# Attention and Fourier mixing on one core: the second batch's key maps, four places for the combinations of w_ch2, and a hold on the third batch's keys

## The chip, the cores and the metric

The kernel runs on one core of a Trainium2 chip. The metric is the device time of one launch in microseconds (us); smaller is better. All arithmetic is in f32.

## The reference, cut to what matters

There are 8 batches (B), 8 heads (H), 576 tokens (S) and a width of 512 (D, 64 per head).

```python
q_s = exp(q - max(q, -1)); q_s /= q_s.sum(-1) + 1e-9        # over the 64 columns of a head
k_s = exp(k - max(k, 2));  k_s /= k_s.sum(2) + 1e-9         # over the 576 tokens
kv  = einsum('bhsd,bhse->bhde', k_s, v)
x   = einsum('bhsd,bhde->bhse', q_s, kv)                    # then heads side by side: (B, S, 512)
u   = x + real(fft(fft(x, axis=1), axis=2))
un  = (u - mean(u)) / sqrt(var(u) + 1e-6)                   # over the 512 columns
out = u + relu(un @ w_ch1) @ w_ch2                          # w_ch1 512 x 2048, w_ch2 2048 x 512
```

`w_ch1` and `w_ch2` arrive as 64-bit floating-point numbers, two 32-bit words each, and the kernel itself turns them into f32. A block of 128 rows by 512 such numbers is called "a word block" below; there are 32 of them, 0 to 15 for `w_ch1` and 16 to 31 for `w_ch2`.

## The kernel before, in words

**One batch.** A batch has two halves. Its *front* is the attention and the Fourier mixing. Keys come in four items per batch (two heads each): `k_load` (L476), the maximum and exponential (`k_exp`, L501), five transposes on TensorE that ScalarE copies to `ks` (`k_turn`, L512), and ten matmul passes whose result goes, scaled, to `kvr` (`k_times_v`, L526). Queries come in four tiles of 128 tokens: exponentials in `q_exp` (L562), transposes in `q_turn` (L584), products with `kvr` in `q_times_kv` (L608), which leaves `x` (L615). The remaining tokens go through `t_turn`, `t_fold` and `t_times_kv`. `transform` (L639) folds the four `x` tiles by sums and differences (`tokens_folded`, `columns_folded`, `by_frequency`, `columns_again`, L648 to L674) and multiplies them by cosine and sine tables in five blocks (`block`, L684; ScalarE copies each result to `Z` and `ZT`, L707 to L712). `second` and `mix_own` (L718, L753) make the second transform and add it to `x`. `norm` (L764) takes the statistics, normalizes, transposes into `unT` and, from batch 1 on, adds the combinations that a Strassen product needs.

The *back* is the two products with `w_ch1` and `w_ch2`. For batch 0 they are plain (`plain`, L826): 16 steps `up(f)` of four matmuls, then 64 steps of `down`, of one matmul each, in the order of `DOWN` (L78). For the later groups they are Strassen products (`strassen`, L854, `up`, `down`), whose combined weights are streamed from DRAM (`w1s`, `w2s`) by `load` (L397). These combinations are made once, beside batch 0's `down`, by `combine` (L366): 8 for `w_ch1`, 8 for `w_ch2`. Each takes sums and differences of four quarters on GpSimd and VectorE, puts the four new quarters in a *place*, and stores them to DRAM by SyncE's DMA queue. For `w_ch2` there are two places in turn, both in `w1sb` (L376).

**Order of the work.** Each batch's front is run beside the back of the one before it. Batch 0's front has nothing to stand beside; neither have batch 1's keys, which are loaded early and handled by `second_keys` (L441), in four items: `maxima`, `exps`, then the pipelined pair `k_turn`, `k_times_v`. L1057 runs, in this order: batch 0's attention, batch 1's maxima and exponentials, batch 0's transform and mixing, batch 1's key products, batch 0's norm. Beside `up` run the conversions of the word blocks; beside the 64 `down` steps run the last conversions, the combinations, and a list `side` with batch 1's queries, transform, mixing and norm. The list `gaps` (L1083) says how many `down` steps lie between two entries of `side`:

```python
side = one + two + norm(1)
gaps = [6] + [4] * (len(one) - 1) + [3] * 5 + [1] * 4 + [2] * (len(two) - 9) + [1] * 7
```

Here `one` has 7 entries (the query pipeline of batch 1) and `two` has 12 (four folds, five blocks, three mixes).

The program is written in this order, but the builder may put an instruction ahead on its engine's queue where it takes it to be ready earlier. The code therefore holds some instructions back by hand: `gate(t, raw)` (L467) and `wait_for` (L257) are tiny VectorE operations that read `t` and rewrite a few elements of `raw` unchanged, so that whatever reads `raw` comes after `t`. `hold` (L264) takes work tiles at the start and frees them later by a tiny copy in `free(f)`; a DMA into such a tile can't be issued before. Batch 2's first key and value tiles are freed after `up(15)`.

**Where word blocks lie.** A fetched word block is raw until converted (`fetch`, `convert`, L313 to L348: two ScalarE operations, two on VectorE, a last one on GpSimd). `WORDS_AT` (L75) gives each one's place: 0 to 7 are pairs of rows of the `w2sb` array, 8 to 10 are tiles that later hold `x`, and 11 to 13 are parts of the tile of `unT`, free once `up` is over. A block whose place was used before is fetched when the former block is converted. The last three blocks (29, 30, 31) are fetched after `up`.

**Keeping TensorE clocked.** In batch 0's folds, `warm` (L201) runs two matmuls into an unused PSUM tile after each of the four `columns_folded` steps (L659); they read the folded tile.

Of the kernel before, what the change touches and what calls it, by code (L numbers as in the profile page):

```python
# [40 lines left out]
F32 = mybir.dt.float32  # L41
# [32 lines left out]

WORDS_AT = [*range(8), 8, 9, 10, *range(3, 8), 0, 1, 2, 8, 9, 10, 4, 5, 6, 7, 8, 9, 10, 11, 12, 13]  # L75
ORDER = (1, 6, 5, 7, 2, 4, 3)
# [20 lines left out]
def pipelined(items, stages):  # L97


    def step(t):  # L100
        for s in range(len(stages) - 1, -1, -1):
            if 0 <= t - s < len(items):
                stages[s](items[t - s])

    return [lambda t=t: step(t) for t in range(len(items) + len(stages) - 1)]
# [17 lines left out]
class _Block:  # L123
# [140 lines left out]
    def hold(self):  # L264


        held = {12: [("q", D, 3)] * 3, 15: [("k", S, 2)] * 2 + [("v", NC * P, 2)] * 2}
        for f, some in held.items():
            for i, (tag, n, bufs) in enumerate(some):
                t = self.work.tile([P, n], F32, tag=tag, name=tag, bufs=bufs)  # L270
                self.nc.gpsimd.memset(t[0:1, 0:1], 0.0)
                some[i] = t[0:1, 0:1]

        def free(f):
            copy = self.nc.vector.tensor_copy
            for t in held.get(f, ()):
                copy(t, self.h0[0:1, f, 0:1])
            if f == NF - 1:
                copy(self.w1sb[0:1, :, 0:1], self.w1sb[0:1, :, 0:1])
        return free  # L280
# [85 lines left out]
    def combine(self, layer, p):  # L366
# [6 lines left out]
        if layer == 0 and p < 2:  # L373
            t = [temp("s1"), temp("u2")] if p == 0 else [temp("u3"), temp("s1")]
        else:
            a = p // 2 * 2 - 2 + NP * (p % 2) if layer == 0 else NP + 2 * (p % 2)  # L376
            t = [pairs(self.w1sb[:, a + i, :]) for i in range(2)]
        quarter = lambda i: w[:, p + NP * (i // 2), (i % 2) * HD:(i % 2 + 1) * HD]
# [11 lines left out]
        nc.sync.dma_start(to[:, second], two)  # L390
        if layer or p > 1:
            nc.sync.dma_start(to[:, 3:], self.w1sb[:, a:a + 2, :].rearrange("p a (s n) -> p (a s) n", s=2))
            return
# [47 lines left out]
    def second_keys(self):  # L441


        nc, V = self.nc, self.nc.vector
        items = [("k", 1, r) for r in range(NR)]
        m, rec = (self.small.tile([P, NR], F32, tag=n, name=n, bufs=1) for n in ("km1", "krec1"))

        def maxima():
            self.gate(self.at_start[2][0][:, 1, :], self.second_at[0][0:1, ::S])
            for it in items:  # L450
                self.k_load(it)
                V.reduce_max(m[:, it[2]:it[2] + 1], self.live[it][0], axis=AX.X, negate=True)
            self.gate(self.xpart(0, 1, 1), m[0:1, :])

        def exps():
            for it in items:
                k, i = self.live[it][0], slice(it[2], it[2] + 1)
                nc.scalar.activation(k, k, ACT.Exp, bias=m[:, i], accum_out=rec[:, i])
                self.live[it].append(rec[:, i])

            t = self.small.tile([P, 1], F32, tag="root", name="root", bufs=1)
            nc.scalar.activation(t[:], rec[:, NR - 1:], ACT.Sqrt)
            V.tensor_scalar(out=rec[:], in0=rec[:], scalar1=ATT_EPS, scalar2=None, op0=ALU.add)
            V.reciprocal(rec[:], rec[:])
        return [maxima, exps], pipelined(items, [self.k_turn, self.k_times_v])

# [172 lines left out]
    def transform(self, b):  # L639
# [14 lines left out]
        def columns_folded(some=range(4)):  # L654
            for i in some:
                e, op = ((V if b == 0 else G), ALU.add) if i < 2 else (V, ALU.subtract)
                t = eo[i]
                e.tensor_tensor(out=t[:, 1:HD], in0=t[:, 1:HD], in1=t[:, D - 1:HD:-1], op=op)
                if b == 0:  # L659
                    self.warm(t[:, 0:HD], 2)  # L660
# [57 lines left out]
    def second(self, z, zr, add):  # L718
# [14 lines left out]
        if self.turns == 1:  # L733

            self.gate(sn[:], self.second_at[0][0:1, ::S])
        two = self.halves()
# [265 lines left out]
def kernel(ctx: ExitStack, tc: tile.TileContext, q, kT, v, w1, w2, ft,  # L1002
# [27 lines left out]
    def norm(g):  # L1030
        def make():
            nexts[g], steps = blk.norm(g)
            return steps
        return late(make, 7)
# [12 lines left out]
    def round_blocks(some):  # L1047
        for i in some:
            convert(i)
            if i in after:  # L1050
                fetch(after[i])
# [3 lines left out]
    one, two = front(0)  # L1055
    keys, products = blk.second_keys()
    for step in one + keys + two + products + norm(0):  # L1057
        step()

    groups = [*range(B - 1), B, B - 1]  # L1060
    for order, g in enumerate(groups):
        loads = [] if g == 0 else None
        one, two = front(order + 1, loads) if order + 1 < B else (blk.later, [])
        if g == 0:
            up, down = blk.plain(0, nexts.pop(0))

            round_blocks(range(4))
            n = 2 * NF - 14
# [8 lines left out]
            for step in loads:  # L1077
                step()
            for i in range(3):
                fetch(2 * NF - 3 + i)  # L1080

            side = one + two + norm(1)
            gaps = [6] + [4] * (len(one) - 1) + [3] * 5 + [1] * 4 + [2] * (len(two) - 9) + [1] * 7  # L1083
            at = 0
# [69 lines left out]
```

## Time and profile before

| what | value |
|---|---|
| median of 3 runs | 1137.43 us (1136.49 to 1137.56) |
| the profiled execution's own time | 1136.85 us |
| its span in the profile | 1135.1 us |
| TensorE (PE) busy | 1096.6 us, 97% |
| VectorE (DVE) / ScalarE (ACT) / GpSimd (POOL) busy | 533.4 / 404.6 / 332.2 us |
| first matmul of `up(0)` (L835) | starts at 65.56 us |
| first matmul of `down` (L844) | starts at 122.15 us |
| last `down` matmul of batch 0 ends | about 198.6 us |
| first matmul of the Strassen part (L905) | starts at 202.09 us |

Positions are microseconds from the start of the profile's span. Engines are PE, PEld (weight loads of TensorE), DVE, ACT, POOL and SP (SyncE, whose queue issues most DMAs; "SPq" is the issue). A row of the timeline reads: start, duration, engine, source line, operation, output<-input, count, and in brackets how long the engine had been idle just before and what released it. "x8" on a row of L835 or L844 are passes: each f32 matmul shows as two. The profiled execution's span leaves 1.75 us of its time outside.

### The profile page before, as it was taken

The numbers are of one execution on the slowest core, as the hardware profiler recorded it, in microseconds if no ns is written. First come the engines' busy times: TensorE is split into PE (matmuls) and PEld (weight loads), VectorE is DVE, ScalarE is ACT, GpSimd is POOL, SyncE is SP. The second block draws the span as 40 slices with busy tenths as digits, with TensorE's granted clock in tenths as the row PEclk, the third lists the DMA queues.
The fourth block names the chain that finished last, engine by engine and source line by source line (L and its number), as shares of the span: only waits on it lengthen the run. The fifth ranks groups of instructions, "written<-read, shape, count | busy, mean of one in ns | idle before, by whom it ended". The sixth has DMA issues, their size and how long they took to land.

```text
span 1135.1 us, 14578 instructions
## 1 busy us (share of the span) xinstructions
PE 1096.6 (97%) x5448; PEld 916.9 (81%) x5448; DVE 533.4 (47%) x1094; ACT 404.6 (36%) x975; POOL 332.2 (29%) x304
## 2 busy tenths in 40 slices
PE   5789999999999999999999999999999999999997
PEld 4644455888888988888889888888889888888886
DVE  6675756368434724384344733592434352203201
ACT  6595523355233513371325322451334152201200
POOL 2055462235003610334024402260034213402320
PEclk9899999999999999999999999999999999999999
DMA  9557675555346534544356425552453344444451
GB/s 312 166 190 227 244 272 161 169 208 167 113 156 215 182 140 144 194 158 177 122 178 220 149 103 183 190 198 107 144 191 150 113 154 160 175 150 151 156 185 55
DMA packets 92549, 193.79 MB, mean 171 GB/s; under 512 B 23088, under 2 KB 59696, under 8 KB 85312
## 3 DMA queue, kind: packets, MB, share of 16 engines
q1 hardware_dynamic: 90680, 191.82, 49.6%
q10 hardware_dynamic: 1800, 1.05, 0.3%
q8 instruction: 43, 0.70, 0.2%
q14 instruction: 26, 0.21, 0.1%
HBM read 168.72 MB, written 28.31 MB: 174 GB/s over the span
## 4 chain that ended last, share of the span: by engine, by line
PE 83%; DVE 4%; DMA 3%; ACT 2%; issue 2%; POOL 1%; SPq 0%; POOLq 0%; ACTq 0%; DVEq 0%
PE bb L905 15%; PE bb L943 15%; PE bc L943 10%; PE ba L943 10%; PE bc L905 10%; PE ba L905 9%; PE acc L531 3%; PE acc L613 2%; PE acc L725 1%; PE acc L701 1%; PE acc L704 1%; DMA w2s<-big 1%; PE bc L844 1%; PE tr L805 1%; PE tr L581 1%
## 5 line engine op out<-in xcount | busy, mean ns | idle before, releaser
L905 PE MATMUL bb<-unT,big 128*128 128x256 f32 x768 | 187.8, 381 | 0.3 <-DVE u L873 0.3
L943 PE MATMUL bb<-big 128*128 128x256 f32 x768 | 172.1, 379 | 0.0
L943 PEld LDWEIGHTS bb<-big 128*128 128x128 f32 x768 | 145.4, 190 | 20.3
L905 PEld LDWEIGHTS bb<-unT,big 128*128 128x128 f32 x768 | 142.8, 190 | 23.5 <-DVE u L873 3.1
L354 POOL TENSOR_TENSOR big<-big 128x512 f32<-128x512 f32 (+1 forms) x38 | 46.4, 1220 | 281.4 <-ACT big L917 273.9
L905 PE MATMUL bc<-unT,big 128*128 128x256 f32 x512 | 125.6, 379 | 0.0
L905 PE MATMUL ba<-unT,big 128*128 128x256 f32 x512 | 123.6, 379 | 0.0
L917 ACT ACTIVATE big<-big 128x512 f32<-128x512 f32 x96 | 60.3, 628 | 173.8 <-DVE big L916 173.5
L943 PE MATMUL bc<-big 128*128 128x256 f32 x512 | 116.0, 379 | 0.5 <-DVE x L960 0.5
L877 DVE TENSOR_TENSOR u<-bb,s 128x512 f32<-128x512 f32 x40 | 27.6, 691 | 186.1 <-PE bb L943 128.3
L943 PE MATMUL ba<-big 128*128 128x256 f32 x512 | 114.8, 379 | 0.0
L943 PEld LDWEIGHTS bc<-big 128*128 128x128 f32 x512 | 96.1, 190 | 14.3 <-DVE x L960 0.9
L943 PEld LDWEIGHTS ba<-big 128*128 128x128 f32 x512 | 95.6, 190 | 12.1
L905 PEld LDWEIGHTS bc<-unT,big 128*128 128x128 f32 x512 | 95.1, 190 | 12.6
L905 PEld LDWEIGHTS ba<-unT,big 128*128 128x128 f32 x512 | 95.0, 190 | 11.8
L362 POOL TENSOR_TENSOR unT<-unT 128x512 f32<-128x512 f32 x8 | 14.2, 1774 | 182.9 <-DVE unT L361 182.9
L570 ACT ACTIVATE q<-q,qm 128x64 f32<-128x64 f32 x240 | 62.1, 339 | 13.8 <-DVE qm L568 13.8
L873 DVE TENSOR_TENSOR u<-bb,s 128x512 f32<-128x512 f32 x40 | 27.6, 690 | 74.3 <-PE bb L905 35.2
L955 POOL TENSOR_TENSOR x<-x,u 128x512 f32<-128x512 f32 x14 | 17.7, 1267 | 147.8 <-DVE u L877 111.2
L916 DVE TENSOR_TENSOR big<-bc,u 128x512 f32<-128x512 f32 x64 | 44.1, 689 | 25.3 <-PE bc L905 24.5
L869 ACT COPY s<-ba 128x512 f32<-128x512 f32 x40 | 23.4, 586 | 88.6 <-PE ba L905 45.5
L809 ACT COPY unT<-tr 128x512 f32<-128x512 f32 x36 | 20.7, 585 | 78.8 <-PE tr L805 78.4
(230 smaller groups left out, 1647.3 us busy)
## 6 DMA issues: line engine op xcount, KB each, us to landing
big<-w1s SPq DMA_DIRECT2D x64, 896.0 KB
big<-w2s SPq DMA_DIRECT2D x56, 1024.0 KB
big<-in_w_dram SPq DMA_DIRECT2D x20, 512.0 KB
q<-in_q_dram SPq DMA_DIRECT2D x27, 256.0 KB
k<-in_kT_dram SPq DMA_DIRECT2D x24, 288.0 KB
v<-in_v_dram SPq DMA_DIRECT2D x24, 256.0 KB
words<-in_w_dram SPq DMA_DIRECT2D x9, 512.0 KB
w2s<-big SPq DMA_DIRECT2D x8, 512.0 KB
```

Of the source, the lines that this page charges most:

```text
L354: e1.tensor_tensor(out=to(4), in0=at(2), in1=at(3), op=ALU.add)
L531: nc.tensor.matmul(pk, lhsT=ks[:, c, :], rhs=v[:, c, :], start=(c == 0), stop=(c == NC - 1))
L570: nc.scalar.activation(heads[:, h, :], heads[:, h, :], ACT.Exp, bias=m[:, h:h + 1])
L613: nc.tensor.matmul(px[:, r * P:(r + 1) * P], lhsT=qT[:, r, :], rhs=self.kvr[b % 2][:, r, :], start=True, stop=True)
L809: nc.scalar.copy(unT[:, u:u + 3:2, :, cols], pt[:].rearrange("p (a k) t -> p a k t", a=2))
L869: nc.scalar.copy(temp("s1"), box["ba"][:])
L873: V.tensor_tensor(out=temp("u2"), in0=box["bb"][:], in1=box["s1"][:], op=ALU.add)
L877: V.tensor_tensor(out=temp("u3"), in0=box["bb"][:], in1=box["s1"][:], op=ALU.add)
L905: nc.tensor.matmul(bank()[:, i, :], lhsT=w[:, WA_AT[m], k * P:(k + 1) * P], rhs=unT[:, B_AT[m], k, :], start=first and i == 0 and k == 0, ...
L916: V.tensor_tensor(out=hp(i), in0=bank[:], in1=u[:], op=ALU.add)
L917: nc.scalar.activation(hp(i), hp(i), ACT.Relu)
L943: nc.tensor.matmul(bank()[:, i, :], lhsT=h[p][:, A_AT[m], i * P:(i + 1) * P], rhs=w[:, p, :], start=first and i == 0 and p == 0, stop=p == ...
```

## The change

Four parts.

1. **Batch 1's keys.** `second_keys` gives back maxima and two groups of steps, items 0 and 1, and items 2 and 3. The first group's exponentials come before batch 0's folds and its products right after the folds; the second group's exponentials come before the last `mix_own`, its products after it. The hold on the exponentials is split: those of items 0 and 1 wait for the last `x` tile, those of items 2 and 3 for the first `sn` (L732). The gate on the keys themselves (L735) goes. The `Sqrt` that loads ScalarE's table comes with the second group.
2. **Smaller holds.** `warm` runs after two of the four column folds. A new gate holds word block 16 until the first part of `unT` is there.
3. **Places.** `WORDS_AT` is changed so that late blocks are 27, 28 and 30 and no `w_ch2` block after 21 lies in places 9 and 10. Combinations of `w_ch2` get four places in turn: two in `w1sb`, the pair of work tiles `s1` and `u2`, and the place of word block 27.
4. **The side list.** Batch 2's key and value tiles are freed by a new entry `free("keys")` after batch 1's mixing, not after `up(15)`; the copies read the last mixed `x`. In `gaps`, the six 4s become 3s.

```diff
-WORDS_AT = [*range(8), 8, 9, 10, *range(3, 8), 0, 1, 2, 8, 9, 10, 4, 5, 6, 7, 8, 9, 10, 11, 12, 13]
+WORDS_AT = [*range(8), 8, 9, 10, *range(3, 8), 0, 1, 2, 8, 9, 10, 4, 5, 6, 7, 8, 11, 12, 7, 13, 8]
+LATE_WORDS = (27, 28, 30)
...
-        held = {12: [("q", D, 3)] * 3, 15: [("k", S, 2)] * 2 + [("v", NC * P, 2)] * 2}
+        held = {12: [("q", D, 3)] * 3, "keys": [("k", S, 2)] * 2 + [("v", NC * P, 2)] * 2}
...
-                copy(t, self.h0[0:1, f, 0:1])
+                copy(t, self.xpart(1, 1, 1)[0:1, 0:1] if f == "keys" else self.h0[0:1, f, 0:1])
...
             a = p // 2 * 2 - 2 + NP * (p % 2) if layer == 0 else NP + 2 * (p % 2)
-            t = [pairs(self.w1sb[:, a + i, :]) for i in range(2)]
+            four = self.w1sb[:, a:a + 2, :].rearrange("p a n -> p (a n)")
+            if layer and p % 4 == 3:
+                four = self.spare_words
+            t = [pairs(four[:, i * D:(i + 1) * D]) for i in range(2)]
+            if layer and p % 4 == 2:
+                t, four = [temp("s1"), temp("u2")], None
...
-            self.gate(self.xpart(0, 1, 1), m[0:1, :])
+            self.gate(self.xpart(0, 1, 1), m[0:1, 0:2])
...
-        return [maxima, exps], pipelined(items, [self.k_turn, self.k_times_v])
+        turned = lambda some: pipelined(some, [self.k_turn, self.k_times_v])
+        return maxima, [lambda: exps(items[:2])] + turned(items[:2]), [lambda: exps(items[2:])] + turned(items[2:])
...
-                if b == 0:
+                if b == 0 and i > 1:
                     self.warm(t[:, 0:HD], 2)
...
-            self.gate(sn[:], self.second_at[0][0:1, ::S])
+            self.gate(sn[:], self.km1[0:1, 2:4])
...
-    keys, products = blk.second_keys()
-    for step in one + keys + two + products + norm(0):
+    maxima, some, others = blk.second_keys()
+    for step in one + [maxima] + some[:1] + two[:1] + some[1:] + two[1:-1] + others[:1] + two[-1:] + others[1:] + norm(0):
...
-            round_blocks(range(4))
+            round_blocks(range(1))
+            blk.gate(unT[:, 0, 0, :], blk.raws[NF][0:1, 0:2])
+            round_blocks(range(1, 4))
...
-            for i in range(3):
-                fetch(2 * NF - 3 + i)
+            for i in LATE_WORDS:
+                fetch(i)
+            blk.spare_words = blk.raws[LATE_WORDS[0]].bitcast(F32)
-            side = one + two + norm(1)
-            gaps = [6] + [4] * (len(one) - 1) + [3] * 5 + [1] * 4 + [2] * (len(two) - 9) + [1] * 7
+            side = one + two + [lambda: free("keys")] + norm(1)
+            gaps = [6] + [3] * (len(one) - 1) + [3] * 5 + [1] * 4 + [2] * (len(two) - 9) + [1] * 8
```

## The prediction

> **What bounds the kernel now.** I read the page's slices first, then the busy time of chosen stretches, the timeline of the start and of batch 0's `down`, and the waits of each engine.
>
> ```profile
> PE   5789999999999999999999999999999999999997
> PEclk9899999999999999999999999999999999999999
> ```
>
> Each digit is a fortieth of the span (28.4 us). TensorE (PE) is full from the third slice on. An edit pays only where it shortens the start, which runs to PE's first `up` matmul, or removes a hole in PE's row later.
>
> ```profile
> core 0: us, PE busy (x) PEld busy (x) DVE busy (x) ACT busy (x) POOL busy (x), PEclk, DMA share, GB/s
> 34.00:46.00 12.00, 10.29 (x49) 8.30 (x48) 7.70 (x23) 7.83 (x25) 1.28 (x1) 0.86 0.58 185
> 50.00:62.70 12.70, 9.39 (x63) 8.27 (x63) 9.08 (x34) 8.39 (x23) 0.00 (x0) 0.87 0.00 1
> ```
>
> In the start no engine is full: it is a chain of latencies. 34 to 46 us is batch 0's folds and blocks, 50 to 62.7 us the key products of batch 1 with the end of the mixing and the norm. The timeline of that second stretch:
>
> ```profile
> 49.48 0.67 ACT L347 ACTIVATE big<-big 128x512 int32<-128x512 uint32 x1 [0.95 <-DMA big<-in_w_dram]
> 50.05 0.56 ACT L518 COPY ks<-tr 128x512 f32<-128x512 f32 x1
> ...
> 53.42 1.27 DVE L774 BATCH_NORM_STATS2 st<-x 128x6 f32<-128x512 f32 x2
> ...
> 57.38 0.30 ACT L778 ACTIVATE std<-mv,eps 128x2 f32<-128x2 f32 x1
> ...
> 62.01 0.63 ACT L537 ACTIVATE kvr<-acc,krec 64x64 f32<-64x64 f32 x2
> ```
>
> ScalarE (ACT) waits 0.95 us for a word block's data with the first `ks` copy behind it. The statistics of the first two tiles end at 53.5 us (their aggregate at 53.20 takes 0.30), but their square root L778 runs at 57.38, because copies for the keys stand before it on ACT. The `ks` copies start at 50.05, 53.48, 56.48 and 59.20: 3.05 us a key. PE's first `up` matmul starts at 65.56.
>
> After that the waits of PE from 66 us on name few places:
>
> ```profile
> PE acc L701 <- ACT ZT L712: 2.7, 1, 2.7
> PE tr L805 <- ACT eo L799: 1.5, 2, 0.9
> PE ba L835 <- ACT unT L809: 1.1, 1, 1.1
> PE tr L517 <- ACT k L507: 1.1, 1, 1.1
> PE tr L581 <- issue: 0.9, 1, 0.9
> PE acc L613 <- ACT qT L588: 0.9, 1, 0.9
> ```
>
> The first is at 180 us:
>
> ```profile
> 174.64 0.79 SPq L487 DMA_DIRECT2D k<-in_kT_dram  x1
> ...
> 178.93 0.77 ACT L507 ACTIVATE k<-k,km 128x576 f32<-128x576 f32 x1 [4.92 <-DVE km L505]
> ...
> 179.70 0.35 ACT L707 COPY Z<-acc 127x256 f32<-127x256 f32 x1
> ...
> 180.28 0.76 PE L701 MATMUL acc<-ft,eo 128*128 128x144 f32 x4 [2.75 <-ACT ZT L712]
> ```
>
> A key of batch 2, not due on PE before 214 us, arrives late. Its exponential stands on ACT ahead of the copies that free PSUM for batch 1's fifth block, so PE waits. The stretches behind it:
>
> ```profile
> 182.00:184.00 2.00, 2.00 (x3) 0.68 (x3) 0.35 (x1) 0.43 (x3) 0.49 (x1) 0.50 0.53 185
> ```
>
> PE runs at half clock (0.76 in the 2 us before, 0.89 in the 2 us after), so the hole costs 2 x (0.24 + 0.50 + 0.11) = 1.7 us more: 4.4 in all.
>
> **What the Trainium skill says.** "TensorE: Matmul & The Clock Gate", What's actually happening: PE's clock is halved after an idle window of about 3.4 us and restored after as long a busy one. The trace agrees in kind: half clock at 182 to 184 us. The hole was 2.75 us, so a shorter one can do it. "PSUM — Partial Sum Buffer", Engine vs sequencer instructions: the queues of ScalarE, VectorE and GpSimd are strictly first in, first out. The trace agrees (178.93, then 179.70). "ScalarE: Activation LUTs", What ACT_TABLE_LOAD costs: a set switch is 1.28 us and a drain of about 1.38; here the row itself takes 1.28 us (L462, at 37.15). It moves with the second group.
>
> **The change, part by part.**
>
> *Keys 0 and 1, beside the folds.* Removed from the tail: two of four keys, 2 x 3.05 = 6.1 us of ACT and PE's alternation. Added between 34 and 46 us on PE: per key five transposes (0.87) and ten passes (1.65), 2 x 2.5 = 5.0 us. Two `warm` calls leave it; they took 1.63 + 1.91 = 3.5 us on PE (rows of L205 at 37.24 and 39.14). Net +1.5 us in a stretch with 12.0 - 10.3 = 1.7 us of PE idle. It also ends a wait of 1.57 us of VectorE (DVE) at 41.09, where L673 could not overwrite what `warm` still read. Last block done: 45.8 us now, 45.3 to 47.9 after (all the alternation's waits exposed); I take 45.8, no change. If that cover is gone it costs 2.1.
>
> *Keys 2 and 3, beside the last sums.* Their two exponentials (2 x 0.79), the table load (1.28) and the root (0.20) may stand before the second `sn` copy (48.16 now) on ACT: 0 to 3.05 us, of which DVE's work on the first `sn` until 49.87 hides 1.4. So 0 to 1.65 on DVE's chain; I take 1.0. Behind these sit the second sums, the statistics and the norm.
>
> *The tail.* DVE's statistics end at 54.7 + 1.0 = 55.7 us. From L778 (57.38) to PE's first `up` (65.56) is 8.2 us now. In it, L342, L347 and key copies occupy ACT from 60.1 to 62.7 while the transposes for `unT` are done at about 61.5; with the keys gone earlier and blocks held, I take 1.2 off. Also the first root starts before the last statistics (at 53.5 + 1.0): 1.2 more at most; I count none. New start: 55.7 - 0.3 + 8.2 - 1.2 = 62.4; with half of that root's lead, 61.8. That is **-3.8 us** (-5.6 to -0.5: both delays at their worst, 2.1 + 1.65, against these gains). The first eight passes took 5.08 us against 3.60 for a warm group, and I leave that as it is. Nothing later in `up` waits: PE is busy 56.44 of 56.5 us, and conversions are gated relative to the norm.
>
> *Small holds.* The gate on block 16 costs one DVE operation of 0.15 us and takes L347's 0.95 + 0.67 from before the first `ks` copy; this is within the tail above. The split reciprocals add two operations of 0.17 on a DVE with idle time. Nothing.
>
> *Third batch's keys held.* The four copies (0.4 us on DVE together) move from 127.5 us to after the mixing. They wait for what DVE itself made. Behind them on SyncE's (SP's) queue are the keys' loads, two of `k` (L487) and four of `v` (L489, L490), about 0.5 us of issue each; next there is a store that waits 15.4 us for `down`'s end anyway (L996). PE wants the first key at 214 us; loads from about 191 us land some 3.5 us after issue (174.64 to the reduction at 178.15), so 15 us of slack cover them. The hole at 180 us goes: **-4.4 us** (-4.4 to 0, where another late entry takes its place).
>
> *Side steps three apart.* Each `down` matmul is 0.857 us (two passes), so batch 1's fold, blocks and mixing come six steps, 5.1 us, earlier against `down`, and the norm five. The norm's last transposes are now behind all of `down`: PE waits 0.95 and 0.53 us there. After, matmuls are left to cover them: **-1.5 us** (0 to -1.5). In return the query steps press on ACT. The first product with `kvr` comes after 13 `down` steps, not 15: 1.7 us earlier. It already waits 0.9 for `qT`, which stood on ACT behind the fourth query's exponentials (132.88 to 134.9) and two word conversions. **+1.8 us** (-0.9 to +4.3, a clock drop of 1.7 with it).
>
> *Four places.* DVE stood 10.4 us at 160.81 for the DMA that read a place, with batch 1's folds behind it; PE's blocks needed them at 170.0, and DVE finished at 169.4. With the steps 5.1 us earlier the blocks want the folds at about 41.5 us after `down`'s start, 47 now. With four places the third and fourth combination no longer wait, and no word block lies where batch 1's `x` goes (ACT waited 4.3 us for L348 there), so `x` and the folds are some 6 us earlier. Zero, with **+0.4** for a partial miss (0 to +6). The DMAs are as many and as large. Blocks 27, 28 and 30, issued after `up`, need their conversion by `down` steps 27, 36 and 38; the late blocks now are converted by about 26 to 30 us after `down`'s start, step 27 is at about 30.
>
> Sum: -3.8 - 4.4 - 1.5 + 1.8 + 0.4 = -7.5 us. From the profiled execution's 1136.85 that is 1129.4; it stands 0.6 below the median, so against the median 1137.43 the forecast is **1129.9 us**.
>
> **Rivals.** (A) *`down` pays back what it gains*: ACT and DVE can't follow the faster side list, and holes of 5.9 us replace those removed. For it: the 0.9 us wait and DVE's 10.4. Against: with four places that wait falls. Only the start is left, 1137.4 - 3.8 = 1133.6.
> (B) *The keys delay the mixing*: PE and ACT alternate in the open, +2.1 at the blocks and +1.65 at the sums; start gain 0.5. For: 1.7 us of idle PE for 1.5 more work. 1137.4 - 0.5 - 3.7 = 1133.2.
> (C) *Slower: the held keys come back at the norm.* The `k` load stands on SP behind the store that waits for `down`'s end (L996; `v` of the second key did, at 199.73), while its maximum stands on DVE before batch 1's statistics. Then DVE waits until about 200 + 3.5 us, and the norm's chain of 11.4 us (191.5 to 202.9) begins only there, while PE runs out of `down` at about 200: 11.4 + 3.5 = 15 us of hole and 1.7 of clock, less the gains of 3.8 + 4.4. 1137.4 + 8.5 = about 1146. It decides once the first key lands more than 11 us after batch 1's last mix. Against it: the loads can be issued 10 us before that store.
>
> **How the numbers follow.** Forecast 0.56 (1125 to 1133.5), A 0.18, B 0.12, C 0.14. Range 1125.0 to 1136.0: the best ends (-5.6 - 4.4 - 1.5 - 0.9 = -12.4) give 1125.0; above it lies C, and below it little. 0.2% (2.3 us) is about what a measurement can tell from no change. Faster by more: 0.56, most of A and B (0.23), so 0.79; within: 0.07; slower: C, 0.14.
>
> **What would show it.** Right: first L835 near 61.8 us, `down` 3.8 us earlier; two `ks` copies before 46 us; no L673 waiting for L205; no L507 ahead of L707 at batch 1's blocks and no half clock there; no wait of L805 for L799 at `down`'s end. Wrong: L701 of batch 1 waiting for DVE's folds, L613 for `qT` over 3 us, or DVE in L505 waiting for a DMA near the norm.

## The result and the profile after

The changed kernel ("after") takes 1138.38 us (median of 4 runs, 1136.87 to 1140.58), the kernel before 1137.1 us (4 runs, 1136.49 to 1137.56). The ratio is 1.0013, 95% interval 0.9995 to 1.0031: no change that a measurement can tell, and 8.5 us above the forecast. The profiled execution of after took 1140.58 us with a span of 1138.8, against 1135.1 before. It is the slowest of after's four, so the two profiles differ by 3.7 us where the medians differ by 1.3.

The slices of after's page:

```profile
PE   5799899899999999999999999999999999999997
PEclk9999999999999999999999999999999999999999
```

The start is better (7, 9 where before had 7, 8), but the fifth and the eighth slice, near 130 and 225 us, are no longer 9s. The waits of PE from 66 us on name what is new (engine, line, what it waited for: us in total, times, longest):

```profile
PE acc L626 <- ACT qT L601: 2.9, 1, 2.9
PE tr L594 <- DVE q L588: 2.7, 2, 2.0
PE tr L594 <- issue: 2.4, 1, 2.4
PE tr L530 <- ACT k L520: 2.3, 1, 2.3
```

The wait for `ZT` at 180 us is gone, and so is that for `eo` at the norm. In their place PE waits for a query (2.9 us, 0.9 before), for a key (2.3 us, 1.1 before), and twice at the turn of a query (2.4 and 2.0, 0.9 and 0.7 before). The key first. DVE's copy that frees its tile (L278), and SP's queue behind it (start, duration, queue and line, operation):

```profile
181.70 0.20 DVE L278 COPY k<-x 1x1 f32<-1x1 f32 x2
...
195.60 0.32 SPq L1009 DMA_DIRECT2D mirror<-x  x1
195.97 0.43 SPq L500 DMA_DIRECT2D k<-in_kT_dram  x1
...
198.43 1.63 SPq L500 DMA_DIRECT2D k<-in_kT_dram  x1
```

Two of batch 0's four result tiles are stored by way of `mirror` on this queue, one near 170 us and one that waits for `down`'s end; "both stores" below and in the recorded texts means these two. In the kernel before, the first key's load stands ahead of both (167.68) and the second's between them (174.64). In after both keys stand behind both stores, 14 us after their tiles came free. The second load is issued at 198.43, in time for a turn at 214 us. But see where that key's maximum stands on DVE:

```profile
222.79 0.69 DVE L929 TENSOR_TENSOR big<-bc,u 128x512 f32<-128x512 f32 x1 [1.03 <-PE bc L918]
223.40 0.74 DVE L518 TENSOR_REDUCE km<-k 128x1 f32<-128x576 f32 x1
224.18 0.78 ACT L520 ACTIVATE k<-k,km 128x576 f32<-128x576 f32 x1
...
225.10 0.66 PE L530 MATMUL tr<-ident,k 128*128 128x128 f32 x4 [2.34 <-ACT k L520]
```

The maximum (L518) is queued behind a sum (L929) that waits for PE's product, and PE's next instruction is the key's turn (L530). PE so waits for a round trip: 0.69 on DVE, 0.74 on DVE, 0.78 on ACT. In the kernel before this key's maximum and exponential were over at 180 us. The clock behind the hole:

```profile
220.00:224.00 4.00, 2.76 (x13) 2.09 (x11) 1.90 (x3) 1.29 (x3) 0.00 (x0) 1.00 0.00 0
224.00:226.00 2.00, 0.82 (x5) 0.53 (x5) 0.50 (x4) 1.22 (x4) 1.70 (x2) 0.92 0.00 0
226.00:228.00 2.00, 1.57 (x7) 1.57 (x8) 1.00 (x2) 1.25 (x3) 2.00 (x2) 0.50 0.45 116
228.00:230.00 2.00, 2.00 (x8) 1.74 (x7) 0.88 (x4) 0.00 (x0) 1.34 (x2) 0.50 0.12 39
230.00:232.00 2.00, 2.00 (x6) 1.58 (x5) 0.00 (x0) 0.00 (x0) 0.00 (x0) 0.50 0.50 143
232.00:234.00 2.00, 2.00 (x13) 1.65 (x12) 0.29 (x1) 0.59 (x1) 0.00 (x0) 0.87 0.54 151
```

Third column from the right is the granted clock: 6 us at 0.50 cost 3.0 us more, and the two stretches beside them 0.4. That is the profiled execution's own share: behind the same hole five other kernels below lose 1.7 us to the clock, not 3.4.

**A table by stage** is what all comparisons below rest on. From the trace of one execution of each kernel I take the start of five instructions: the first `up` matmul, the first `down` matmul, the first product of the Strassen parts (L905 before, L918 after), and the copies of the third, sixth, fourteenth and fifteenth `s` on ACT (L869 before, L882 after). "Keys" is from that first product to the third copy, "queries" from the third to the sixth, "14-15" between those two copies. From the sixth to the fourteenth it is 168.7 us in every kernel, and after the fifteenth 616.3 to 617.0. Times in us; the ratio is of measured times against the kernel before on the same chip.

| run | first `up` | `up` | `down` | keys | queries | 14-15 | ratio (95% interval) |
|---|---|---|---|---|---|---|---|
| before | 65.56 | 56.59 | 79.94 | 33.97 | 91.78 | 22.21 | 1 |
| after | 61.41 | 57.26 | 77.29 | 40.03 | 93.78 | 23.55 | 1.0013 (0.9995 to 1.0031) |
| e3_start_alone | 62.34 | 55.92 | 79.58 | 33.97 | 91.85 | 22.22 | 0.9983 (0.9971 to 0.9994) |
| e2_hold_alone | 63.59 | 56.22 | 74.56 | 38.58 | 91.63 | 22.33 | 0.9998 (0.9983 to 1.0013) |
| v_two_nohold | 63.26 | 56.71 | 81.39 | 37.83 | 92.28 | 22.22 | 1.0046 (1.0030 to 1.0061) |
| e6_exp_late | 63.49 | 55.01 | 77.57 | 33.97 | 91.82 | 22.25 | 0.9965 (0.9952 to 0.9977) |
| e9_key_queue | 62.97 | 56.71 | 78.70 | 34.49 | 93.92 | 22.22 | 1.0000 (0.9985 to 1.0015) |
| e1_no_hold | 62.52 | 57.58 | 75.61 | 38.80 | 93.49 | 25.23 | 1.0002 (0.9985 to 1.0020) |
| p_gaps3 | 64.10 | 57.03 | 77.28 | 37.78 | 92.28 | 22.22 | 1.0008 (0.9992 to 1.0024) |
| p_places | 64.17 | 61.60 | 74.72 | 38.32 | 92.28 | 22.34 | 1.0031 (1.0020 to 1.0042) |
| e16_hold_queue | 63.45 | 56.20 | 78.07 | 35.60 | 91.61 | 22.22 | 0.9997 (0.9985 to 1.0008) |
| e14_start_hold_queue | 62.57 | 55.22 | 78.59 | 34.46 | 91.62 | 23.66 | 0.9966 (0.9953 to 0.9978) |
| e15_exp_after_norm | 63.99 | 55.01 | 75.12 | 33.98 | 92.60 | 23.56 | **0.9936 (0.9920 to 0.9952)** |
| e18_after_keys_mended | 62.81 | 56.70 | 77.19 | 34.50 | 95.02 | 22.21 | 0.9992 (0.9980 to 1.0004) |
| e19_gaps3_keys_mended | 62.59 | 55.01 | 79.07 | 34.12 | 93.92 | 23.56 | 0.9977 (0.9966 to 0.9988) |
| e20_places_keys_mended | 62.15 | 55.47 | 76.22 | 34.50 | 93.64 | 25.23 | 0.9981 (0.9970 to 0.9992) |

Against before, after's profile gains 4.15 us at the start and 2.65 in `down`; it loses 0.67 in `up`, 6.06 at the keys, 2.00 at the queries, 1.34 in 14-15 and 0.5 behind: +3.7 in all. These are differences of two executions; 1.7 of the 6.06 us is the longer spell of low clock just named.

### The profile page after: what moved, and what is told of

It reads as the page before. It is cut to its first block, busy times and chain, and to the rows that moved or that the text cites. A ratio compares the mean times of both kernels' runs of the same rounds, so it can differ in the third digit from the quotient of the medians.

```text
span 1138.8 us, 14563 instructions
## 1 busy us (share of the span) xinstructions
PE 1097.0 (96%) x5440; PEld 918.6 (81%) x5440; DVE 540.2 (47%) x1097; ACT 404.8 (36%) x975; POOL 334.9 (29%) x304
## 4 chain that ended last, share of the span: by engine, by line
PE 88%; ACT 3%; DVE 2%; DMA 2%; issue 2%; POOL 1%; SPq 0%; ACTq 0%; POOLq 0%
PE bb L918 15%; PE bb L956 15%; PE bc L956 10%; PE ba L956 10%; PE bc L918 9%; PE ba L918 9%; PE acc L544 3%; PE acc L626 3%; PE bc L857 2%; PE acc L714 2%; PE acc L717 2%; PE acc L738 2%; PE tr L594 1%; PE tr L818 1%; PE tr L530 1%
## 5 line engine op out<-in xcount | busy, mean ns | idle before, releaser
L918 PE MATMUL bb<-unT,big 128*128 128x256 f32 x768 | 189.7, 384 | 0.2 <-DVE u L886 0.2
L918 PEld LDWEIGHTS bb<-unT,big 128*128 128x128 f32 x768 | 143.8, 192 | 24.0 <-DVE u L886 2.6
L355 POOL TENSOR_TENSOR big<-big 128x512 f32<-128x512 f32 (+1 forms) x38 | 46.4, 1220 | 273.6 <-ACT big L930 273.6
L918 PE MATMUL bc<-unT,big 128*128 128x256 f32 x512 | 125.3, 379 | 0.0
L918 PE MATMUL ba<-unT,big 128*128 128x256 f32 x512 | 124.5, 382 | 0.2 <-ACT unT L822 0.2
L918 PEld LDWEIGHTS ba<-unT,big 128*128 128x128 f32 x512 | 95.7, 191 | 12.3 <-ACT unT L822 0.5
L918 PEld LDWEIGHTS bc<-unT,big 128*128 128x128 f32 x512 | 95.3, 190 | 12.6
L929 DVE TENSOR_TENSOR big<-bc,u 128x512 f32<-128x512 f32 x64 | 44.1, 689 | 27.2 <-PE bc L918 26.4
L882 ACT COPY s<-ba 128x512 f32<-128x512 f32 x40 | 23.4, 585 | 90.7 <-PE ba L918 46.5
```

What stands on the lines that cost most here:

```text
L355: e1.tensor_tensor(out=to(4), in0=at(2), in1=at(3), op=ALU.add)
L882: nc.scalar.copy(temp("s1"), box["ba"][:])
L918: nc.tensor.matmul(bank()[:, i, :], lhsT=w[:, WA_AT[m], k * P:(k + 1) * P], rhs=unT[:, B_AT[m], k, :], start=first and i == 0 and k == 0, ...
L929: V.tensor_tensor(out=hp(i), in0=bank[:], in1=u[:], op=ALU.add)
```

## The experiments

The theory that I tested first, called "second key": the gains are real and are given back because batch 2's keys now stand behind the store on SP. Against it stood "pace" (what PE gains early, ACT and DVE take back anyway) and, by parts, "places", "hold" and "steps".

**The start alone (e3_start_alone).** Parts 1 and 2 of the change; `WORDS_AT`, the places, the hold of batch 2's keys and `gaps` stay as before.

```diff
-    for step in one + keys + two + products + norm(0):
+    for step in one + [maxima] + some[:1] + two[:1] + some[1:] + two[1:-1] + others[:1] + two[-1:] + others[1:] + norm(0):
...
-                if b == 0:
+                if b == 0 and i > 1:
```

> Before with the start alone changed: keys of the second batch two and two, warm calls two fewer, the gates on block 16, on sn and on the last part of x; keys not held, two places, steps four apart. Theory 'second key' (the start's gain and the gain at 180 us are real, and are given back where batch 2's second key arrives late, because its load now stands behind the store that waits for down's end): that load is issued as early as in the kernel before, so nothing is given back: first up matmul about 61.4 us, 1133.3 us, with the 2.75 us hole at 180 us still there. Rival 'pace' (what PE gains early, ACT, DVE or a chance drop of the clock take back later, whatever the keys do): no hole names a key, yet the time ends at 1136.5 us or more.

Measured 1134.53 us, ratio 0.9983. The keys' stretch is 33.97 us, to the hundredth that of before, and `ZT` is still waited for at 180 us (2.5 us). "Second key" holds in the place, not in the size: the gain is 0.17% (0.06 to 0.29), some 1.9 us, and not 4.1.

**The hold alone (e2_hold_alone).** On the kernel before:

```diff
-        held = {12: [("q", D, 3)] * 3, 15: [("k", S, 2)] * 2 + [("v", NC * P, 2)] * 2}
+        held = {12: [("q", D, 3)] * 3, "keys": [("k", S, 2)] * 2 + [("v", NC * P, 2)] * 2}
...
-            side = one + two + norm(1)
+            side = one + two + [lambda: free("keys")] + norm(1)
```

> Before with the hold alone: the third batch's keys are freed after the second batch's last mix, not after the sixteenth up step. Theory 'second key': the hole at 180 us goes (-4.4), the second key's turn comes late and PE waits about 2.3 us there, with some 3.5 us lost to a lower clock (+5.8), so about 1137 to 1139 us. Rival 'places' (the hold is harmless, the four places and the steps three apart make the loss): 1133 us, no hole at a key.

Measured 1135.30 us, ratio 0.9998, a little below the range of "second key"; in time the hold's gain and loss nearly cancel. Both halves of the hold are seen at once: `down` is 5.4 us shorter, the hole at 180 us gone, and the keys' stretch 4.6 us longer, with the same hole at the second key:

```profile
222.91 0.73 PE L517 MATMUL tr<-ident,k 128*128 128x128 f32 x4 [2.31 <-ACT k L507]
```

**After without hold and with two places (v_two_nohold).**

```diff
-            if layer and p % 4 == 3:
-                four = self.spare_words
...
-            if layer and p % 4 == 2:
-                t, four = [temp("s1"), temp("u2")], None
```

and the hold back at `up(15)`.

> After with two places instead of four and without the hold (start, new order of the word blocks and steps three apart are kept). The first key's load stands between the two stores on SyncE's queue, the second behind both. Theory 'second key': the second key is still late, a hole of 1 to 2.5 us at its turn near 225 us, 1134 to 1138 us. Rival 'places': without the four places and the hold the loss of 7.5 us is gone, 1131 to 1133 us.

Measured 1140.88 us, ratio 1.0046: worse than either theory gave. The key's wait of 2.3 us is there without hold and without four places (keys 37.83), which leaves the steps three apart, the word blocks' new order and the new start. `down` is longer than before, with a wait of 5.1 us for `Z` at batch 1's mixing (L738).

**Early keys, late exponentials (e6_exp_late).** The start alone, and in `k_exp`:

```diff
         V.reduce_max(m[:], k, axis=AX.X, negate=True)
+        if it[1] == 2 and it[2] < 2:
+            self.gate(self.xpart(1, 1, 1)[0:1, 0:1], m[0:1, :])
```

> The start alone, with one thing more: batch 2's first two keys are loaded as early as in the kernel before, but their exponentials are made to depend on the second batch's last mix (a one-element operation of DVE on the negated maximum). Theory 'second key': the start's -4.1 and the hole's -4.4 both come and nothing is given back, 1128.9 us; no wait of the fifth block for ACT at 180 us, no half clock behind it, first up matmul at 61.4 us. Rival 'pace': at least half of the 8.5 us comes back as other holes, 1133 us or more.

Measured 1132.50 us, ratio 0.9965. The keys' stretch stays at 33.97 and the hole at 180 us is gone, but of its 4.4 us `down` keeps only 2.0 against the start alone (77.57, 79.58). In time some 4 of the 8.5 us came, so more than half was given back, as "pace" had it, though at a place that can be named. PE now waits for the norm:

```profile
PE tr L814 <- ACT eo L808: 3.2, 3, 2.0
```

ACT's timeline says why. The two exponentials (L516) stand ahead of the norm's `eo`, one on each side of its square root, so that both table loads lie between them as well:

```profile
186.84 0.78 ACT L516 ACTIVATE k<-k,km 128x576 f32<-128x576 f32 x1 [2.93 <-DVE km L480]
...
187.73 1.28 ACT L787 ACT_TABLE_LOAD   x1
189.02 0.30 ACT L787 ACTIVATE std<-mv,eps 128x4 f32<-128x4 f32 x1
189.34 1.28 ACT L516 ACT_TABLE_LOAD   x1
190.63 0.78 ACT L516 ACTIVATE k<-k,km 128x576 f32<-128x576 f32 x1
...
191.50 1.50 ACT L808 ACTIVATE eo<-x,mv,std 128x512 f32<-128x512 f32 x2
```

**The disputed cause by itself (e9_key_queue).** After, with one line changed:

```diff
-        nc.sync.dma_start(k, self.kT[b, r * P:(r + 1) * P, :])
+        (nc.gpsimd if b == 2 and r < 2 else nc.sync).dma_start(k, self.kT[b, r * P:(r + 1) * P, :])
```

> After with one edit: the loads of batch 2's first two keys (k alone, their v stay) are issued from GpSimd's queue, where no store waits for down's end; everything else, the hold too, is as in after. Theory 'second key': both keys come in time, the second key's maximum no longer stands behind the first sums of the later parts on DVE, the holes near 225 and 256 us and the half clock go, and 5 to 7 of the 7.5 us lost between 211 and 277 us come back: 1131 to 1134 us. Rival 'pace' (four places and steps three apart lose it wherever the key is loaded): 1136.5 us or more, with holes of the same sum at other instructions.

Measured 1136.40 us, ratio 1.0000.

```profile
182.61 1.22 POOL L500 DMA_DIRECT2D k<-in_kT_dram  x2 [10.92 <-DVE k L278]
...
215.09 0.60 PE L530 MATMUL tr<-ident,k 128*128 128x128 f32 x4
```

For this stretch the mechanism is shown: with the same hold, places and steps, the two keys are turned at 210.84 and 215.09 us (208.84 and 225.10 in after), neither turn is waited for, the clock stays at 1.00 from 222 to 234 us, and the keys' stretch falls from 40.03 to 34.49. In time the run misses its range: it stands beside "pace", and its ratio is not clearly apart from after's 1.0013, since the intervals overlap. Two reasons are seen. The queries' stretch keeps its 2 us, with the hole of 2.2 us near 253 us that I had expected to go. And the freed load meets the norm, where a maximum of the key now stands among batch 1's statistics and waits for its data:

```profile
187.61 0.75 DVE L518 TENSOR_REDUCE km<-k 128x1 f32<-128x576 f32 x1 [1.81 <-DMA k<-in_kT_dram]
188.28 0.17 DVE L788 BATCH_NORM_AGGREGATE mv<-st 128x2 f32<-128x6 f32 x1
188.37 0.66 DVE L787 BATCH_NORM_STATS2 st<-x 128x6 f32<-128x512 f32 x1
```

`down` is 1.4 us longer than in after. That is rival C's place, at a small price.

**After without the hold (e1_no_hold).**

```diff
-        held = {12: [("q", D, 3)] * 3, "keys": [("k", S, 2)] * 2 + [("v", NC * P, 2)] * 2}
+        held = {12: [("q", D, 3)] * 3, 15: [("k", S, 2)] * 2 + [("v", NC * P, 2)] * 2}
```

> After without the hold: the third batch's keys are freed after the sixteenth up step, as in the kernel before; start, four places and steps three apart are kept. The loads still stand behind both stores on SyncE's queue. Theory 'second key': what places the load is its place on that queue, not when the tile is free, so the same hole of about 2.3 us at the second key near 225 us: 1137.5 to 1139.5 us, as after. Rival 'hold' (it is the hold by itself that makes the key late): 1131 to 1133 us.

Measured 1136.23 us, ratio 1.0002. The key's hole stays (2.35 us at 224.90, keys 38.80). The rival "hold" falls as the only cause. The median is lower than I gave; the profiled execution, at 1140.41 us, was among the kernel's slowest, so its stretches, not its span, are used here.

**Steps three apart alone (p_gaps3)**, on the kernel before:

```diff
-            gaps = [6] + [4] * (len(one) - 1) + [3] * 5 + [1] * 4 + [2] * (len(two) - 9) + [1] * 7
+            gaps = [6] + [3] * (len(one) - 1) + [3] * 5 + [1] * 4 + [2] * (len(two) - 9) + [1] * 7
```

> Before with the steps three apart alone (two places, no hold, old start). The first key's load then stands between the two stores, the second behind both, as in the run with two places and without the hold. Theory 'second key': late second key (hole 2.3 us and lower clock, +5.8), and a wait of about 5 us at batch 1's blocks in place of 2.75, less the norm's 1.5: 1139 to 1143 us. Rival 'places' (steps three apart are harmless by themselves): 1135 to 1137 us.

Measured 1137.65 us, ratio 1.0008. The key's hole is there (2.34 us, keys 37.78), against the rival; in time the run lies between the two forecasts, and no loss is told from none. The new wait, at batch 1's mixing, is 2.1 us and not 5, and `down` is 2.7 us shorter.

**Four places and the word blocks' order alone (p_places)**, on the kernel before:

```diff
-WORDS_AT = [*range(8), 8, 9, 10, *range(3, 8), 0, 1, 2, 8, 9, 10, 4, 5, 6, 7, 8, 9, 10, 11, 12, 13]
+WORDS_AT = [*range(8), 8, 9, 10, *range(3, 8), 0, 1, 2, 8, 9, 10, 4, 5, 6, 7, 8, 11, 12, 7, 13, 8]
+LATE_WORDS = (27, 28, 30)
...
+            if layer and p % 4 == 3:
+                four = self.spare_words
```

> Before with the four places and the word blocks' new order alone (steps four apart, no hold, old start). Both keys' loads then stand behind both stores. Theory 'second key': late second key (+5.8), hole at 180 us gone since its exponentials now come later (-4.4 to 0): 1138 to 1143 us. Rival 'steps' (the four places are harmless, steps three apart alone lose the time): 1133 to 1137 us.

Measured 1140.32 us, ratio 1.0031: slower. The key's hole again, 2.34 us (keys 38.32). And a wait that no theory had, in `up`, for a word block's conversion, with the next eight passes taking 6.38 us where a group of eight takes 3.60:

```profile
112.69 6.38 PE L841 MATMUL bb<-unT,big 128*128 128x512 f32 x8 [3.65 <-ACT big L843]
```

So the hold, the steps and the places each push the second key's load behind both stores, and each gives the same hole. No two of them are needed together, and the start alone leaves that load between the two stores (169.54).

**The hold and the key's queue (e16_hold_queue)**, on the kernel before: the edits of the hold alone and of the disputed cause.

> Before with the hold alone and, as the one further edit, batch 2's first two k loads on GpSimd's queue instead of SyncE's. Theory 'second key': the hold's gain in down (74.6 us from the first down matmul to the later parts' first product, where the kernel before had 79.9) stays, and the stretch from there to the third sum's copy falls from 38.6 us to the 34.0 that it has where the keys are loaded early: some 5 us below the kernel before, ratio about 0.9955. Rival 'pace': the stretch stays at 37 us or more with other holes, ratio 0.999 or above.

Measured 1136.51 us, ratio 0.9997: a miss. The ratio is the rival's, the stretch is neither's. The keys' stretch falls to 35.60, but `down` gives back 3.5 of its 5.4 us. As with the late exponentials, ACT has an exponential before the norm's square root and one behind it (two table loads of 1.28 us), and PE waits 2.84 us for `eo`.

**Start, hold and queue together (e14_start_hold_queue)**: the start alone with those two edits.

> The new start, the hold, and batch 2's first two k loads on GpSimd's queue; two places, steps four apart as before. Theory 'second key': the start's gain (first up matmul between 61.4 and 63.5 us), a down of about 74.6 us and the later stretch of 34.0 to 34.5 us add up: 6 to 7 us below the kernel before, ratio about 0.994, the fastest version. Rival 'next late' (a PE that is earlier by the start finds the norm late, as with the late exponentials, so the two gains don't add): 3 to 4 us below, ratio 0.9965.

Measured 1133.36 us, ratio 0.9966: the number of "next late". PE waits 2.96 us for `eo` at the norm, and `down` takes 78.59. But its reason, that the new start makes PE early for the norm, doesn't hold: the run before this one has the old start, the same wait (2.84 us) and a `down` of 78.07. The norm is late by the exponentials and table loads in both, and the new start's gain is kept (0.9966 against 0.9997).

**Exponentials after the norm (e15_exp_after_norm).** As with the late exponentials, but the gate reads the last part of batch 1's `unT` (kept as `unT1` in `norm`):

```diff
+            self.gate(self.unT1[:, 3, 1, P:P + 1][0:1, :], m[0:1, :])
```

> The new start with early loads of batch 2's first two keys; their exponentials now depend on the last part of the norm's transposed output, not on the last mix. Theory 'exponentials ahead of the norm' (in the run with late exponentials their two times 0.8 us stood on ACT ahead of the norm, so the hole removed at 180 us came back as 3.2 us of waits for the norm): those waits fall to about 1.5 us, down takes 75 to 76 us in place of 77.6, ratio about 0.995. Rival 'mix' (the norm is late because DVE's mixing is): down stays at 77 to 78 us, ratio 0.9965, as with the late exponentials.

Measured 1130.34 us, ratio 0.9936 (0.9920 to 0.9952): the fastest version, faster than both kernels (six executions; the profiled one, at 1131.50, is the slowest). `down` takes 75.12 us, `eo` is waited for 1.5 us, and on ACT the norm's first `eo` starts 2.55 us earlier. The exponentials are behind it, and the square root's table is loaded at 184.22, while ACT has nothing else to do:

```profile
188.95 1.50 ACT L810 ACTIVATE eo<-x,mv,std 128x512 f32<-128x512 f32 x2
...
195.72 0.78 ACT L516 ACTIVATE k<-k,km 128x576 f32<-128x576 f32 x1 [0.82 <-DVE km L480]
```

**After with its keys mended (e18_after_keys_mended)**: no hold, the `k` loads on GpSimd's queue, and that gate; start, places and steps kept.

> After with its keys mended: no hold, batch 2's first two k loads early from GpSimd's queue, their exponentials made to depend on the norm's last output as in the fastest run so far; the start, the four places with the word blocks' new order, and the steps three apart are kept. Theory 'second key' in its wide form (the late key and the key's exponentials ahead of the norm are all that is wrong with the change): the stretch from the later parts' first product to the third sum's copy is 34.0 us, down 74 to 76 us, ratio 0.991 to 0.995. Rival 'the rest costs too' (four places and steps three apart bring their own waits, at batch 1's queries and at the third query of batch 2): the stretch is mended but down or the stretch to the sixth sum's copy is 2 us or more longer than in the fastest run, ratio 0.996 or above.

Measured 1135.26 us, ratio 0.9992, 0.56% above the fastest version. The rival's numbers are right: against that version `up` is 1.7, `down` 2.1 and the queries' stretch 2.4 us longer. In that stretch this execution lost 3.4 us to the clock behind the third query's turn (0.65, 0.50, 0.50, 0.65 from 250 to 258 us), where the next two runs lost 1.7.

```profile
PE acc L628 <- ACT qT L603: 2.8, 2, 2.3
PE tr L596 <- issue: 2.2, 1, 2.2
```

The last two runs split this.

```diff
-            gaps = [6] + [4] * (len(one) - 1) + [3] * 5 + [1] * 4 + [2] * (len(two) - 9) + [1] * 7
+            gaps = [6] + [3] * (len(one) - 1) + [3] * 5 + [1] * 4 + [2] * (len(two) - 9) + [1] * 7
```

on the fastest version, with the `k` loads on GpSimd's queue (e19_gaps3_keys_mended):

> The fastest version (new start, early keys with their exponentials after the norm) with the steps three apart added, and its two k loads on GpSimd's queue, so that they aren't pushed behind the stores. Theory 'steps' (the steps three apart bring the queries' wait in down and nothing else): up 55 us, the wait of 1.5 to 2.5 us for qT near 133 us is there, down 76 to 78 us, the stretch to the sixth sum's copy 92 us; ratio 0.995 to 0.998. Rival 'places' (the whole residue comes from the four places): as the fastest version, ratio 0.993 to 0.995.

Measured 1134.06 us, ratio 0.9977, in the range of "steps", with `down` and the queries' stretch (93.92) longer than given. With the steps there are three waits of over 1 us for `qT`, and `down` is 4.0 us longer than in the fastest version:

```profile
130.83 1.16 PE L622 MATMUL acc<-kvr,qT 128*128 128x128 f32 x8 [1.47 <-ACT qT L597]
139.97 1.16 PE L622 MATMUL acc<-kvr,qT 128*128 128x128 f32 x8 [1.06 <-ACT qT L597]
146.16 1.76 PE L622 MATMUL acc<-kvr,qT 128*128 128x128 f32 x8 [2.02 <-ACT qT L597]
```

And after with its keys mended, with the steps four apart again (e20_places_keys_mended):

> After's keys mended, with steps four apart again: new start, early keys, exponentials after the norm, four places with the word blocks' new order. Theory 'steps': the queries' wait near 133 us is 0.9 us or less and down about 75 us; the 1.7 us in up, which come from the word blocks' order, stay: ratio 0.995 to 0.997. Rival 'places': the query's waits near 133 and 250 us stay, ratio 0.998 or above.

Measured 1134.74 us, ratio 0.9981. A wait of 1.75 us for `qT` at 132.84 stays, so "steps" is wrong there, and the 1.7 us in `up` that it kept are not (55.47). The wait is there with the steps and with the places, and each run is some 0.4% above the fastest version. Both together were 0.56% above, less than twice that, and four places alone on the kernel before left this wait at 0.9 us. Both runs also have the key's loads on another queue than the fastest version has, and both have the third query's wait of 2.2 us; how much of the cost is that queue's is not told apart.

## Why the prediction was wrong

**The hold: right in its gain, wrong in its cover; here the sum failed.** "The hole at 180 us goes: -4.4" held: 5.4 us off `down` in the hold alone. The step that failed is "loads from about 191 us land some 3.5 us after issue (174.64 to the reduction at 178.15), so 15 us of slack cover them". It failed twice. The prediction had the loads ahead of the store; they stood behind it, and tiles that were free at 182 us were loaded from 195.97 and 198.43. That alone was still in time: the first key's maximum ran 3.1 us after its load's issue, and the second key's, when its turn came, waited for no DMA. But the slack was worth nothing. It was counted from landing to turn, as if the key's maximum and exponential ran when their data was there. They stand in queues whose order is written when the program is built. With the load behind a store that waits for `down`'s end, the builder also put the maximum behind a sum that waits for PE. "PSUM — Partial Sum Buffer", Engine vs sequencer instructions, had said strict first in, first out, and the prediction quoted it for ACT and did not apply it to DVE. Measured in place of zero: 6.1 us in after (1.7 of it the longer spell of low clock), 3.8 to 4.8 in five other kernels with the key behind both stores, 0.5 in after once the key's queue was changed.

**Four places: not zero plus 0.4.** Two costs were missed. The builder, with the places changed, set both stores ahead of both keys, also without any hold. And the word blocks' new order made PE wait 3.65 us in `up` where it is alone (at most 0.6 with the new start). With the keys mended the part costs about 0.45% (0.9981 against 0.9936), with the reserve on the queue named above. (The forecast's 41.5 us for the folds comes to 42.7 from its own 170.0, 122.15 and 5.1; nothing hung on it.)

**The start: right in kind, mis-sized.** -3.8 was expected and the two profiles show -4.1. Over all profiles it is -1.4: the old start has its first `up` at 65.56, 63.59, 64.10, 64.17 and 63.45 us (mean 64.2), the new one in eleven executions from 61.41 to 63.99 (mean 62.7). The pair that I had was the extreme of both. The new start was forecast at 61.8, 0.9 below its mean; the other 1.4 us of the error lie in the base, 65.56 against 64.2. And the sum took half of the first root's lead, 0.6 us, after it had counted none; without that it gives 62.4. In the profile before, two `warm` groups ran at a lower clock (38 to 44 us: 0.74) and took 1.63 and 1.91 us, and this made L673 wait 1.57 us. The same groups in the hold alone, the start being the same:

```profile
36.98 1.10 PE L205 MATMUL tr<-eo,ident 128*128 128x256 f32 x4 [0.51 <-DVE eo L658]
38.16 1.06 PE L205 MATMUL tr<-eo,ident 128*128 128x256 f32 x4
```

L673 waits for nothing there. After's own profile had the better luck, 1.00 at 50 to 56 us where six other new starts have 0.68 to 0.87. The steps themselves: the last block ends at 46.93 (45.8 given), two `ks` copies come before 46 us, and the second `sn` copy is 2.4 us later (50.53; 0 to 3.05 given). The version with the start alone gained 1.9 us; that much of the forecast stood.

**The norm's transposes** lost their wait for `eo` (-1.5, right), and **the queries** pressed as given: 2.92 us in after, 0.9 before, +2.0 for +1.8.

**What no step named.** The third turn of a query: in before PE has four products (1.13 us) to run ahead of it, made possible by a sum (L873) that DVE does before the query's scale (L575); in after both orders are the other way round, the turn comes first, and PE waits 2.4 us for the scale (L588), with the clock at 0.60 and 0.55 behind it: +2.0. Before, then after:

```profile
253.49 0.68 DVE L873 TENSOR_TENSOR u<-bb,s 128x512 f32<-128x512 f32 x1
254.22 1.13 PE L905 MATMUL bb<-unT,big 128*128 128x256 f32 x4 [0.28 <-DVE u L873]
256.29 0.63 PE L581 MATMUL tr<-ident,q 128*128 128x128 f32 x4 [0.94 <-issue]
...
254.46 1.59 DVE L588 TENSOR_TENSOR q<-q,qrec 128x512 f32<-128x512 f32 x1
255.97 0.68 DVE L886 TENSOR_TENSOR u<-bb,s 128x512 f32<-128x512 f32 x1
256.15 0.86 PE L594 MATMUL tr<-ident,q 128*128 128x128 f32 x4 [2.38 <-issue]
```

This too goes with the key's load: the hole is 0.94 us in the four kernels that load both keys early on SP's queue (before, e3, e6 and e15) and 1.7 to 2.4 us in the twelve others, the hold alone with two places and steps four apart among them. How the builder comes from one to the other was not tested. Where the clock stays up behind a hole of 2.38 us (v_two_nohold, p_gaps3, p_places) the stretch is only 0.5 us longer than before; the other 1.5 us in after come with the clock.

And 1.3 us between the fourteenth and fifteenth copy, where one operation of DVE meets GpSimd at another moment. This comes and goes between versions (22.2, 23.6 or 25.2 us) and I found no part of the change that sets it.

**The rivals.** C had the mechanism, a key's load behind the store, and looked for the damage at the norm. In after the norm was free and the damage came 25 us later; the norm was hit only where the load was freed, 1.8 us. A (holes in `down`) did not come: `down` is 2.65 us shorter. B (the keys delay the mixing) came in part: the last block is 1.1 us and the second `sn` copy 2.4 us later, and the start's gain lies between B's 0.5 and the forecast's 3.8. No change within 0.2%, which is what came, had been given 0.07. The sign of C, that DVE waits in the key's maximum for a DMA near the norm, did not look for a maximum that waits in a queue.

Stays open: how much of 0.4% each the places and the steps cost by themselves, apart from the key's queue, and what makes the builder reorder the third query's turn.

## What to carry to other kernels

When a load is moved, do not count slack from its landing: find where each of its followers will stand on its engine, and what the instruction ahead of it waits for. A freed stall is worth only what the next stage can take: several versions removed the same hole, and what they kept depended largely on whether two exponentials stood before or behind the norm. And take the size of a latency chain from several executions, since one profile can carry 2 us of clock luck.

## What the runs showed of the hardware

- At the places named here the clock took its share in steps of 1.7 us: what is missing from the granted clock, summed over stretches of 2 us, as 2 x (0.29 + 0.50 + 0.06) behind the key's hole in e1 from 226 to 232 us. The hole of 2.75 us in before and the key's holes of 2.3 us in e1, e2, v_two_nohold, p_gaps3 and p_places were each followed by 1.7 us of loss, the key's hole in after by 3.4. At the third query's turn a hole of 2.38 us brought 1.7 us in after and in e1, and none in v_two_nohold, p_gaps3 and p_places: the length of a hole alone does not decide. "TensorE: Matmul & The Clock Gate", What's actually happening, gives an idle window of about 3.4 us and says that it runs free of the kernel. These holes are shorter; 1.7 us is what one such window at half clock would cost, an estimate from that page's figure. After and after without the hold have the same start, and ran its 50 to 56 us at 1.00 and at 0.73.
- DVE slows beside GpSimd. In after the 128x8 scalar operation of a query took 0.17 us at 249.84 and 1.23 at 252.96, and its 128x512 product 0.69 and 1.59, the longer ones while GpSimd ran L355 to L357. "SBUF — State Buffer", Who interferes with whom, says that the two share a pair of ports under an exclusive lock; the trace agrees in kind. In the kernel before the same two operations are as slow (1.24 us at 252.34, 1.53 at 254.66), so this lengthens PE's wait in both kernels and is not what tells them apart; the order is.
- A table load between `Exp` and `Sqrt` took 1.28 us on ACT each time, as "ScalarE: Activation LUTs", What ACT_TABLE_LOAD costs, states. With the two exponentials around the square root, one of these loads no longer fell into idle time, and the norm began 2.55 us later, not the 1.6 of the exponentials alone.
